# A chunked attention and two feed-forward layers: blocks cut by batch, additions on another engine, copies later

## The chip, the cores and the metric

The kernel runs on one core of a Trainium2 chip. Its engines are TensorE (PE; PEld is its weight load), VectorE (DVE), ScalarE (ACT), GpSimd (POOL) and SyncE (SP), which here only issues transfers. The metric is the device time of one execution in microseconds (us).

## The reference

For 8 batches, 8 heads, 576 tokens and 64 numbers a head, attention is computed within chunks of 64 tokens. Its output x, 4608 tokens by 512, goes through two feed-forward layers of width 2048. All is float32.

```python
scores = scale * np.matmul(q_c, k_c.transpose(0, 1, 2, 4, 3))
...
attn = attn / (np.sum(attn, axis=-1, keepdims=True) + 1e-09)
out = np.matmul(attn, v_c)
...
r = np.maximum(h, 0.0)
g = s * (r * r) + b
return (g @ w_out).astype(np.float32)
...
g = h * (1.0 / (1.0 + np.exp(-1.702 * h)))
return (g @ w_out).astype(np.float32)
```

## The kernel before

Every float32 operand is split into a high and a low part, and a product is three matmuls (high by high, high by low, low by high). `split` makes the parts: ScalarE copies the high one (L102), VectorE subtracts it (L103).

The 4608 tokens are cut into 9 blocks of 512. As a batch has 576 tokens, most blocks cross from one batch into the next, and `runs` gives the pieces. A block goes through attention in four pairs of heads (class `Pair`): loads of q and k (L294) and v (L304) on SP's queue, one for each run, transposes on VectorE (L311 for q and k, L320 for p), matmuls, and the softmax (mx L359, p L360 and L364, sm L366 to L368, p L369). L339 stores x of a block that comes later in a pair of blocks.

Blocks 0 to 6 then go singly through the first layer: `gemm_in` (matmuls L554; ScalarE's L566 takes h from PSUM, L567 squares it, L102 and L103 split it into gh and gl) and `gemm_out` (L629). One block goes singly through the second layer (L569 to L572 in place of L566 and L567). All others are computed in pairs of blocks by the class `Halves`, a scheme that needs 7 products in place of 8, in which some weight operands are sums of quarters of the weights. These sums lie in DRAM in `wi_sums` and `wo_sums`, together with copies of three quarters (`copies`, L263).

The second layer's weights come in 64 bits a number and are decoded by `decode_second`: integer operations on ScalarE, VectorE (L127, L130) and GpSimd (L128), a store to DRAM on GpSimd's queue (L203), then `add_quarters` (L221 to L224, four additions of 128x256), a split (ScalarE L209, VectorE L211) and stores on SP (L213). `sums` does the same for the first layer's weights (L240, `add_quarters`, L247, L252, stores L254). Both write their sums to a staging buffer `wst`, of which there are three. `second_weights` loads the decoded weights back (wm, L228) and splits them into resident buffers (ScalarE L150, VectorE L151).

The order is made in two steps. `at(t, f)` puts a piece of work on a list with a time t; 32 units are one block's stage, and the pieces are traced in the order of t. A scheduler then orders each engine's instructions by its own estimate. `behind` makes an instruction wait for a marked one. Each engine runs its instructions strictly in its order. SP has eight transfers in flight at most, since its transfers take eight semaphores in turn.

Of the kernel before, what the change touches and what calls it, by code (L numbers as in the profile page):

```python
# [11 lines left out]
ALU = mybir.AluOpType  # L12
# [4 lines left out]
P = 128  # L17
CH = 64
# [7 lines left out]
LAG = 2  # L26
# [11 lines left out]

PLACE = {"M1": 0, "M2": 1, "M4": 2, "M5": 3, "M6": 4, "M7": 5, "M3": 6}
BANK = {"M1": "x", "M6": "x", "M7": "x", "M4": "x", "M5": "d", "M3": "d", "M2": "b"}  # L40
PAIRS = ((1, 1), (0, 7), (1, 3), (1, 5), (1, 7))
OUT_ORDER = ("M1", "M5", "M6", "M2", "M7", "M3", "M4")


# [1 line left out]
def chunk_attention_two_ffn(ctx, tc, q, k, v, w1_in, w1_out, s, b, w2_in, w2_out, out):  # L46
# [17 lines left out]
    NB_MAX = 512  # L64
    sizes = [512] * 9
    assert sum(sizes) == NT
    starts = [sum(sizes[:i]) for i in range(len(sizes))]
    NBLK = len(sizes)
    PAIRED = [j + c for f, j in PAIRS if f == 0 for c in range(2)]
    SINGLE = NBLK - len(PAIRED)  # L70

    const = ctx.enter_context(tc.tile_pool(name="const", bufs=1))
# [142 lines left out]
    def add_quarters(kind, s, tiles):  # L215

        one, two = tiles
        a11, a22 = one[:, 0, :], two[:, 1, :]
        a12, a21 = (one[:, 1, :], two[:, 0, :]) if kind == "wi" else (two[:, 0, :], one[:, 1, :])
        s1, s2, s3, s4 = (s[:, t, :] for t in range(4))  # L220
        nc.gpsimd.tensor_tensor(out=s1, in0=a21, in1=a22, op=ALU.add)  # L221
        nc.gpsimd.tensor_tensor(out=s3, in0=a11, in1=a21, op=ALU.subtract)
        nc.gpsimd.tensor_tensor(out=s2, in0=s1, in1=a11, op=ALU.subtract)
        nc.gpsimd.tensor_tensor(out=s4, in0=a12, in1=s2, op=ALU.subtract)  # L224

    def second_weights(kind, i):
        m = tmp("wm")
# [37 lines left out]

    def runs(j):

        c0, n = starts[j] // CH, sizes[j] // CH
        done = 0
        while done < n:  # L270
            bb, c = divmod(c0 + done, CPB)
            step = min(n - done, CPB - c)
            yield done, step, bb, c
            done += step

    heads = [slice(h * CH, (h + 1) * CH) for h in range(2)]

    class Pair:
# [160 lines left out]
    class Early:  # L439
# [4 lines left out]
            self.raw, self.v = {}, {}  # L444

        def load(self, to, src, i, h0, nh):
            t0 = starts[self.j] + i * P
            done = 0
            while done < P:
                bb, t = divmod(t0 + done, S)  # L450
                n = min(P - done, S - t)
                nc.sync.dma_start(
                    out=to[done:done + n, h0 * D:(h0 + nh) * D].rearrange("p (h d) -> p h d", d=D),
                    in_=src[bb, h0:h0 + nh, t:t + n, :].rearrange("h p d -> p h d"),
                )
                done += n

        def load_qk(self, h0, nh):
            for x, src in (("q", q), ("k", k)):
# [65 lines left out]
        steps_at(((o - 2, 3), (o + 1, 1), (o + 2, 4), (o + 8, 1), (o + 8.5, 1)), pr.steps)  # L525

    def plan_y(j):
        base = NS * (SINGLE + j - 1)
        n = sizes[j]
        st = {}  # L530

        def load(m):
            st[m] = tmp("yst")[:, 0:n]
            nc.sync.dma_start(out=st[m], in_=y_dram[j][:, m, :])

        def sp(m):
# [77 lines left out]
    def gemm_out(f, j, i, g):  # L614
        n = sizes[j]
        gh, gl = g
        hi, lo = W[f, "wo", i]
        na = KD if f == 0 else n // P
        if i == 0:
            for m in range(na):  # L620
                acc[m] = acc_ps.tile([P, n if f == 0 else DM], F32, tag=f"acc{m}", name=f"acc{m}")
        for m in range(na):
            sl = slice(m * P, (m + 1) * P)
            if f == 0:
                prods = ((lo[:, sl], gh), (hi[:, sl], gh), (hi[:, sl], gl))
            else:
                prods = ((gl[:, sl], hi), (gh[:, sl], hi), (gh[:, sl], lo))
            for a, (l_, r_) in enumerate(prods):
                nc.tensor.matmul(  # L629
                    out=acc[m], lhsT=l_, rhs=r_, start=i == 0 and a == 0, stop=i == KF - 1 and a == 2  # L630
                )
        if i == KF - 1:
            if f == 0 and j == 0:
                make_shift()
            for m in range(na):
                w = n if f == 0 else DM
                st = tmp("ost")[:, 0:w]
                add = shift[:, m:m + 1]
                if f == 0 and m % 2:
                    nc.vector.tensor_scalar(  # L640
                        out=st, in0=acc[m], scalar1=s_ap, scalar2=add, op0=ALU.mult, op1=ALU.add
                    )
                elif f == 0:
                    nc.scalar.activation(out=st, in_=acc[m], func=AF.Identity, scale=s_ap, bias=add)
                elif m % 2:
                    nc.vector.tensor_copy(out=st, in_=acc[m])
                else:
                    nc.scalar.copy(out=st, in_=acc[m])
                if f == 0:
                    nc.sync.dma_start(out=y_dram[j][:, m, :], in_=st)  # L650
                else:
                    t0 = starts[j] + m * P
                    nc.sync.dma_start(out=out[t0:t0 + P, :], in_=st)


    HF, HK = KF // 2, KD // 2
# [4 lines left out]
    class Halves:  # L661


        def __init__(self, f, j, base):
            self.f, self.j, self.base = f, j, base
            self.last = (f, j) == PAIRS[-1]
            self.x, self.w, self.g, self.op, self.ps, self.kept = {}, {}, {}, {}, {}, {}


        def load_x(self, k):  # L670
            self.raw = getattr(self, "raw", {})
            for (a, c) in ((0, 0), (0, 1), (1, 1), (1, 0)):
                t = tmp("xr")
                nc.gpsimd.dma_start(out=t, in_=(y_dram if self.f else x_dram)[self.j + c][:, k + a * HK, :])  # L674
                self.raw[k, a, c] = t

        def x_place(self, n):
# [47 lines left out]
        def first(self, i, m):  # L725
            key = i, BANK[m]
            start = key not in self.ps
            if start:
                self.bank(key, BANK[m], f"acc{i % KD}")
            w = self.wi[i][PLACE[m]]  # L730
            for k in range(HK):
                xh, xl = self.x[m, k]
                hi, lo = w[:, k, 0, :], w[:, k, 1, :]
                for a, (l_, r_) in enumerate(((lo, xh), (hi, xh), (hi, xl))):
                    nc.tensor.matmul(  # L735
                        out=self.ps[key], lhsT=l_, rhs=r_,
                        start=start and k == 0 and a == 0, stop=k == HK - 1 and a == 2,
                        skip_group_check=not start,
                    )
            if m == "M4" and i == HF - 1:  # L740
                marks["last first product", self.f, self.j] = latest(mybir.EngineType.PE)

        def keep(self, key, name):
            self.kept[key[0], name] = t = tmp("kept")
# [80 lines left out]
        def second(self, n, i, zs=(0, 1)):  # L825
# [14 lines left out]
                        skip_group_check=not start,  # L840
                    )
            if n == 0 and i == 3:
                behind(old, mybir.EngineType.PE, ("last first product", self.f, self.j))

        def keep_out(self, z, bank, name):
            self.kept[z, name] = t = tmp("kept")
# [2 lines left out]
        def result(self, name, z):  # L849
# [7 lines left out]
            if self.f == 0:  # L857
                m = (int(name[0]) - 1) * HK + z
                y = tmp("ost")
                nc.scalar.activation(out=y, in_=c, func=AF.Identity, scale=s_ap, bias=shift[:, m:m + 1])  # L860
                nc.sync.dma_start(out=y_dram[self.j + int(name[1]) - 1][:, m, :], in_=y)
                return
            o = tmp("ost").rearrange("p (u l) -> p u l", l=BK)
            nc.vector.transpose(out=o, in_=c.rearrange("p (u l) -> p u l", l=BK))
            t0 = starts[self.j + int(name[1]) - 1]
# [99 lines left out]
    plan_first_products()  # L965
    for j in range(2, NBLK):
        plan_attention(j)
    plan_y(0)
# [5 lines left out]
    for i in range(KF):  # L974
        for n, kind in enumerate(("wi", "wo")):
            t = NS * (SINGLE - 1) + 2 * i + 1 + 3 * n
            at(t, second_weights, kind, i)
            if i >= KF // 2:
                at(t + 3, copies, 1, kind, i - KF // 2)
    def first_product(*a):  # L980
        G[a] = gemm_in(*a)

    for z in range(2, SINGLE + 1):
        f, j = divmod(z, SINGLE)
# [3 lines left out]
    for n, (f, j) in enumerate(PAIRS):  # L988
        Halves(f, j, NS * (SINGLE + 1) + 2 * LAG + 56 * n).plan()
# [33 lines left out]
```

## Time and profile before

| what | value |
|---|---|
| median of three runs | 1634.05 us (1632.6 to 1637.57) |
| the profiled execution's own time | 1637.07 us |
| its span | 1635.3 us |
| mean granted clock of TensorE | 0.985 |
| VectorE busy | 1126.0 us, 69% |
| ScalarE busy | 823.1 us, 50% |
| GpSimd busy | 252.0 us, 15% |

The span is the time from the first to the last instruction of the profiled execution. Busy times are sums over instructions. The granted clock is 1 at TensorE's higher level and 0.5 at its lower one. The times in the rows further down count from the span's start.

### The profile page before, as it was taken

The numbers are of one execution on the slowest core, as the hardware profiler recorded it, in microseconds if no ns is written. First come the engines' busy times: TensorE is split into PE (matmuls) and PEld (weight loads), VectorE is DVE, ScalarE is ACT, GpSimd is POOL, SyncE is SP. The second block draws the span as 40 slices with busy tenths as digits, with TensorE's granted clock in tenths as the row PEclk, the third lists the DMA queues.
The fourth block names the chain that finished last, engine by engine and source line by source line (L and its number), as shares of the span: only waits on it lengthen the run. The fifth ranks groups of instructions, "written<-read, shape, count | busy, mean of one in ns | idle before, by whom it ended". The sixth has DMA issues, their size and how long they took to land.

```text
span 1635.3 us, 24857 instructions
## 1 busy us (share of the span) xinstructions
PE 1584.5 (97%) x8840; PEld 1296.5 (79%) x8840; DVE 1126.0 (69%) x1836; ACT 823.1 (50%) x1427; POOL 252.0 (15%) x286
## 2 busy tenths in 40 slices
PE   7889998999999999999999999999999999999998
PEld 5668886778888888787888888888888888888886
DVE  5667668768777776766754697359468946984685
ACT  3766424445444555555233564776346525653552
POOL 1344214234333333200100000010001000100000
PEclk7999999999999999999999999999999999999999
DMA  9757667666665566799615777687668686877764
GB/s 231 227 171 206 202 170 216 167 178 173 186 173 160 165 203 162 231 284 294 189 47 163 222 252 196 201 270 212 204 194 273 184 220 210 259 199 207 217 202 76
DMA packets 392395, 326.73 MB, mean 200 GB/s; under 512 B 256592, under 2 KB 330320, under 8 KB 392272
## 3 DMA queue, kind: packets, MB, share of 16 engines
q1 hardware_dynamic: 382096, 301.81, 65.5%
q0 software_dynamic: 5760, 18.88, 3.4%
q10 hardware_dynamic: 4416, 4.46, 0.8%
q8 instruction: 70, 1.15, 0.3%
q14 instruction: 53, 0.43, 0.1%
HBM read 232.78 MB, written 92.27 MB: 199 GB/s over the span
## 4 chain that ended last, share of the span: by engine, by line
PE 52%; DVE 4%; DMA 3%; issue 1%; ACT 1%; SPq 1%; POOL 1%; DVEq 0%; POOLq 0%; ACTq 0%
PE x L735 13%; PE x L837 13%; PE d L735 7%; PE d L837 7%; PE b L837 3%; PE b L735 3%; PE acc L629 3%; PE h L554 3%; DMA wm<-w_wi 1%; DVE pt L320 1%; DMA wm<-w_wo 1%; DVE wi L151 0%; DVE gl L103 0%; SPq L263 0%; PE xT L330 0%
## 5 line engine op out<-in xcount | busy, mean ns | idle before, releaser
L554 PE MATMUL h<-xh,wi 128*128 128x512 f32 x1024 | 326.1, 400 | 18.3 <-ACT r L585 8.6
L629 PE MATMUL acc<-gh,wo 128*128 128x512 f32 x896 | 278.7, 395 | 3.5 <-ACT gh L102 3.5
L554 PEld LDWEIGHTS h<-xh,wi 128*128 128x128 f32 x1024 | 193.1, 192 | 61.5 <-ACT r L585 9.4
L554 PE MATMUL h<-xl,wi 128*128 128x512 f32 x512 | 202.4, 396 | 0.0
L629 PEld LDWEIGHTS acc<-gh,wo 128*128 128x128 f32 x896 | 167.4, 189 | 39.5 <-ACT gh L102 4.0
L629 PE MATMUL acc<-gl,wo 128*128 128x512 f32 x448 | 173.4, 393 | 2.4 <-DVE gl L103 2.4
L813 ACT ACTIVATE op<-wo 128x512 fp32r<-128x512 f32 x160 | 100.0, 630 | 101.4 <-PE x L837 34.4
L837 PE MATMUL x<-op,wi 128*128 128x512 f32 x540 | 130.2, 389 | 0.0
L735 PE MATMUL x<-xh,wi 128*128 128x512 f32 x400 | 124.1, 391 | 3.1 <-DVE wo L756 3.1
L814 DVE TENSOR_TENSOR op<-wo,op 128x512 fp32r<-128x512 f32 x160 | 108.5, 685 | 19.7 <-ACT op L813 18.1
L837 PEld LDWEIGHTS x<-op,wi 128*128 128x128 f32 x540 | 101.4, 188 | 21.0
L554 PEld LDWEIGHTS h<-xl,wi 128*128 128x128 f32 x512 | 98.1, 192 | 21.4 <-DVE xl L103 0.3
L659 DVE TENSOR_TENSOR wo<-wo 128x512 f32<-128x512 f32 x160 | 107.9, 687 | 4.5 <-ACT wo L759 3.7
L763 DVE TENSOR_TENSOR wo<-wo,r 128x512 f32<-128x512 f32 x96 | 66.0, 691 | 65.0 <-ACT r L762 64.6
L128 POOL TENSOR_TENSOR wm<-wm,wc 128x512 int32<-128x512 int32 x52 | 73.1, 1408 | 211.2 <-DVE wm L127 95.5
L674 POOL DMA_DIRECT2D xr<-y x32 | 17.5, 548 | 561.5 <-DVE op L814 274.4
L629 PEld LDWEIGHTS acc<-gl,wo 128*128 128x128 f32 x448 | 84.3, 189 | 21.6 <-DVE gl L103 3.9
L813 ACT ACTIVATE gh<-wo 128x512 fp32r<-128x512 f32 x120 | 75.1, 630 | 52.2 <-PE x L837 18.9
L320 DVE STREAM_TRANSPOSE pt<-p 32x256 f32<-32x256 f32 x224 | 97.6, 436 | 3.9
L762 ACT ACTIVATE r<-wo 128x512 f32<-128x512 f32 x96 | 60.7, 632 | 75.9 <-DVE wo L756 75.1
L814 DVE TENSOR_TENSOR gl<-wo,gh 128x512 fp32r<-128x512 f32 x120 | 80.9, 688 | 19.0 <-ACT gh L813 13.4
L735 PEld LDWEIGHTS x<-xh,wi 128*128 128x128 f32 x400 | 74.7, 188 | 20.4 <-DVE wo L756 5.2
(162 smaller groups left out, 3030.1 us busy)
## 6 DMA issues: line engine op xcount, KB each, us to landing
wi<-wo_sums SPq DMA_DIRECT2D x140, 512.0 KB, 4.3
wi<-wi_sums SPq DMA_DIRECT2D x120, 512.0 KB, 3.8
wst<-in_moe_w_out SPq DMA_DIRECT2D x32, 512.0 KB, 4.1
wst<-in_moe_w_in SPq DMA_DIRECT2D x24, 512.0 KB, 4.4
wi_sums<-wi SPq DMA_DIRECT2D x48, 256.0 KB, 4.0
wo_sums<-wo SPq DMA_DIRECT2D x48, 256.0 KB, 3.9
wi<-wi_sums SPq DMA_DIRECT2D x40, 256.0 KB, 3.6
y<-ost SPq DMA_DIRECT2D x36, 256.0 KB, 3.6
```

Of the source, the lines that this page charges most:

```text
L128: nc.gpsimd.tensor_tensor(out=t, in0=t, in1=c.bitcast(I32), op=ALU.add)
L320: nc.vector.transpose(out=pt[r.start + ek * BK:r.start + (ek + 1) * BK, :, eq * BK:(eq + 1) * BK], in_=p[r.start + eq * BK:r.start + (eq + ...
L554: nc.tensor.matmul(out=ps, lhsT=w_[:, kk, :], rhs=x_, start=kk == 0 and a == 0, stop=kk == KD - 1 and a == 2,)
L629: nc.tensor.matmul(out=acc[m], lhsT=l_, rhs=r_, start=i == 0 and a == 0, stop=i == KF - 1 and a == 2)
L659: nc.vector.tensor_tensor(out=to, in0=one, in1=two, op=ALU.subtract)
L674: nc.gpsimd.dma_start(out=t, in_=(y_dram if self.f else x_dram)[self.j + c][:, k + a * HK, :])
L735: nc.tensor.matmul(out=self.ps[key], lhsT=l_, rhs=r_, start=start and k == 0 and a == 0, stop=k == HK - 1 and a == 2, skip_group_check=not ...
L762: nc.scalar.activation(out=r, in_=h, func=AF.Sigmoid, scale=1.702)
L763: nc.vector.tensor_tensor(out=g, in0=h, in1=r, op=ALU.mult)
L813: nc.scalar.activation(out=hi, in_=src, func=AF.Copy)
L814: nc.vector.tensor_tensor(out=lo, in0=src, in1=hi.bitcast(F32), op=ALU.subtract)
L837: nc.tensor.matmul(out=self.ps[key], lhsT=l_, rhs=r_, start=start and i == 0 and a == 0, stop=i == HF - 1 and a == 2, skip_group_check=not ...
```

## The change

The change has three parts.

1. Blocks are cut otherwise. Block 1 (`LEFT`) takes the last chunk of each batch, eight runs of one chunk; each other block is the first 512 tokens of one batch, one run. A pair of heads in blocks 2 to 7 is loaded with 10 transfers in place of 20, of the same bytes in all: 6 blocks by 4 pairs by 10 are 240 issues fewer on SP. Block 1, loaded at the program's start, takes 24 transfers of 64 rows in place of 15. Block 1, not block 0, goes singly through the second layer, and its result is stored in pieces of 64 rows.
2. The four additions of `add_quarters` run on VectorE, not on GpSimd. It is called 32 times.
3. The 48 copies of the second layer's weights (256 KB each) are no longer made as the weights come in, but in the stage after, in four groups of 12; each group waits on SP behind the store of block 8's x for one pair of heads.

A line n of the kernel before is line n + 1 or a little more after.

```diff
-PAIRS = ((1, 1), (0, 7), (1, 3), (1, 5), (1, 7))
+PAIRS = ((1, (0, 2)), (0, (7, 8)), (1, (3, 4)), (1, (5, 6)), (1, (7, 8)))
...
+    LEFT = 1
...
-        nc.gpsimd.tensor_tensor(out=s1, in0=a21, in1=a22, op=ALU.add)
-        nc.gpsimd.tensor_tensor(out=s3, in0=a11, in1=a21, op=ALU.subtract)
-        nc.gpsimd.tensor_tensor(out=s2, in0=s1, in1=a11, op=ALU.subtract)
-        nc.gpsimd.tensor_tensor(out=s4, in0=a12, in1=s2, op=ALU.subtract)
+        nc.vector.tensor_tensor(out=s1, in0=a21, in1=a22, op=ALU.add)
+        nc.vector.tensor_tensor(out=s3, in0=a11, in1=a21, op=ALU.subtract)
+        nc.vector.tensor_tensor(out=s2, in0=s1, in1=a11, op=ALU.subtract)
+        nc.vector.tensor_tensor(out=s4, in0=a12, in1=s2, op=ALU.subtract)
...
-        c0, n = starts[j] // CH, sizes[j] // CH
-        done = 0
-        while done < n:
-            bb, c = divmod(c0 + done, CPB)
-            step = min(n - done, CPB - c)
-            yield done, step, bb, c
-            done += step
+        if j == LEFT:
+            for bb in range(B):
+                yield bb, 1, bb, CPB - 1
+        else:
+            yield 0, NB_MAX // CH, first_batch(j), 0
+
+    def first_batch(j):
+        return j - (j > LEFT)
...
+                marks["stored", self.j, self.hp] = latest(mybir.EngineType.SP)
...
-                    t0 = starts[j] + m * P
-                    nc.sync.dma_start(out=out[t0:t0 + P, :], in_=st)
+                    for r, bb in zip(heads, (2 * m, 2 * m + 1)):
+                        t0 = bb * S + NB_MAX
+                        nc.sync.dma_start(out=out[t0:t0 + CH, :], in_=st[r])
...
-            if i >= KF // 2:
-                at(t + 3, copies, 1, kind, i - KF // 2)
+    for n, (kind, i) in enumerate((kind, i) for kind in ("wi", "wo") for i in range(KF // 2)):
+
+        def later(kind=kind, i=i, p=n // HP):
+            old = len(nc.cur_bb.bb.instructions)
+            copies(1, kind, i)
+            behind(old, mybir.EngineType.SP, ("stored", NBLK - 1, p))
+        at(NS * SINGLE + 7 * (n // HP) + 5.6 + 0.1 * (n % HP), later)
```

The order on VectorE, at the ninth of the 16 decodes (kind wi), where L211 splits the sums of the second layer and the sums of the first layer follow; gl, xl, mx and p belong to the blocks' work. Before:

```order
L103 TENSOR_TENSOR gl<-r,gh 128x512 [waits PE_49,Activation_49]
L211 TENSOR_TENSOR wst<-wst 128x1024 [waits Activation_49]
L103 TENSOR_TENSOR gl<-r,gh 128x512 [waits PE_49,Activation_49]
L103 TENSOR_TENSOR xl<-xT,xh 128x512 [waits Activation_49]
L359 TENSOR_REDUCE mx<-sc 128x8 [waits PE_49]
L360 TENSOR_TENSOR p<-sc,mx 128x512 [waits DMAHW6_49,DVE_49]
L366 TENSOR_REDUCE sm<-p 128x8 [waits Activation_49]
L252 TENSOR_TENSOR wst<-wst,vs 128x512 [waits DMAHW1_49,Activation_49,Pool_49]
```

And now:

```order
L225 TENSOR_TENSOR wst<-wm,wst 128x256 [waits DVE_49]
L212 TENSOR_TENSOR wst<-wst 128x1024 [waits Activation_49]
L104 TENSOR_TENSOR gl<-r,gh 128x512 [waits PE_49,Activation_49]
L222 TENSOR_TENSOR wst<-vs 128x256 [waits DMAHW4_49,DVE_49]
L223 TENSOR_TENSOR wst<-vs 128x256
L224 TENSOR_TENSOR wst<-wst,vs 128x256 [waits DVE_49]
L104 TENSOR_TENSOR xl<-xT,xh 128x512 [waits Activation_49]
L362 TENSOR_REDUCE mx<-sc 128x8 [waits PE_49]
L225 TENSOR_TENSOR wst<-vs,wst 128x256 [waits DVE_49]
L253 TENSOR_TENSOR wst<-wst,vs 128x512 [waits DVE_49,Activation_49]
```

The additions L222 to L225 now stand in this queue; the first of them waits for a transfer (DMAHW4), the store of the staging buffer that L212 wrote two rows ahead, and xl, mx and all behind stand after it.

The order on SP where the second weights are loaded, from the last store of the last sums on; w_wo_117 is the second of the output weights' tiles. Before:

```order
L254 DMA wo_sums_148<-wst 128x2x256
L294 DMA ks<-in_k 32x14x32
L339 DMA x_150<-xo 128x512
L294 DMA ks<-in_k 32x14x32 x2
L294 DMA qs<-in_q 32x2x32 x4
L294 DMA ks<-in_k 32x2x32 x4
L304 DMA vs<-in_v 64x7x64 x2
L304 DMA vs<-in_v 64x64
L228 DMA wm<-w_wo_117 128x512
L228 DMA wm<-w_wi_103 128x512
```

And now:

```order
L255 DMA wo_sums_148<-wst 128x2x256
L341 DMA x_150<-xo 128x512
L296 DMA ks<-in_k 32x16x32
L306 DMA vs<-in_v 64x8x64 x6
L229 DMA wm<-w_wo_117 128x512
L229 DMA wm<-w_wi_103 128x512
```

The loads of the second run of each block are gone from ahead of the weights' loads, and the weights stand nearer to the stores.

## Rows read from the trace of the kernel before

**Rows 1.** The page's part on engines: busy us (share of the span) xinstructions.

```profile
PE 1584.5 (97%) x8840; PEld 1296.5 (79%) x8840; DVE 1126.0 (69%) x1836; ACT 823.1 (50%) x1427; POOL 252.0 (15%) x286
```

**Rows 2.** PE's waits in 255 to 400 us: us in total, times, longest.

```profile
PE h L554 <- ACT r L566: 7.1, 3, 4.4
PE acc L629 <- DVE gl L103: 2.4, 2, 1.4
```

**Rows 3.** PE's waits in 661 to 775 us.

```profile
PE acc L629 <- ACT gh L102: 3.5, 1, 3.5
PE h L554 <- DVE r L570: 1.5, 1, 1.5
PE xT L330 <- DVE pt L320: 0.9, 1, 0.9
```

**Rows 4.** Windows: length, busy us of PE, PEld, DVE, ACT, POOL, clock, DMA share, GB/s.

```profile
275.00:300.00 25.00, 20.62 (x133) 15.88 (x133) 24.54 (x30) 10.55 (x18) 12.50 (x15) 0.86 0.75 198
287.20:294.10 6.90, 4.92 (x12) 3.86 (x13) 6.62 (x15) 3.67 (x7) 0.00 (x0) 0.51 0.87 246
686.60:693.40 6.80, 6.10 (x24) 4.36 (x26) 6.64 (x10) 4.07 (x8) 2.66 (x4) 0.50 0.93 267
693.40:768.50 75.10, 73.14 (x482) 59.61 (x478) 46.99 (x85) 38.81 (x67) 2.30 (x2) 1.00 1.03 298
768.50:775.30 6.80, 6.02 (x24) 4.40 (x25) 5.77 (x10) 4.12 (x8) 0.00 (x0) 0.50 0.77 207
775.00:850.00 75.00, 75.00 (x512) 61.90 (x509) 47.67 (x86) 23.50 (x41) 4.40 (x8) 1.00 0.44 136
```

**Rows 5.** Timeline of VectorE, 276 to 288 us: start, length, instruction.

```profile
276.76 4.23 DVE L103 TENSOR_TENSOR gl<-r,gh 128x512 fp32r<-128x512 f32 x1
...
287.29 0.69 DVE L360 TENSOR_TENSOR p<-sc,mx 128x512 f32<-128x512 f32 x1
```

**Rows 6.** Timeline of ScalarE at 285 us, idle time before in brackets.

```profile
285.54 1.06 ACT L209 ACTIVATE wst<-wst 128x1024 fp32r<-128x1024 f32 x1 [3.95 <-POOL wst L224]
```

**Rows 7.** VectorE's instructions grouped by form: count, busy us, mean ns.

```profile
L814 DVE TENSOR_TENSOR gl<-wo,gh 128x512 fp32r<-128x512 f32 x120 | 80.9, 688 | 19.0 <-ACT gh L813 13.4 <-PE x L837 3.7 <-PE b L837 0.7
L103 DVE TENSOR_TENSOR gl<-r,gh 128x512 fp32r<-128x512 f32 x80 | 70.9, 890 | 9.7 <-ACT gh L102 9.6
...
L103 DVE TENSOR_TENSOR xl<-xT,xh 128x256 fp32r<-128x256 f32 x16 | 6.3, 417 | 4.2 <-ACT xh L102 4.2
```

**Rows 8.** Timeline of ScalarE at 686 us.

```profile
686.10 0.63 ACT L150 ACTIVATE wo<-wm 128x512 fp32r<-128x512 f32 x1 [4.75 <-DMA wm<-w_wo]
```

**Rows 9.** Timeline of SP, 674 to 683 us: issues.

```profile
674.58 0.51 SPq L294 DMA_DIRECT2D ks<-in_k  x1
...
682.90 0.53 SPq L228 DMA_DIRECT2D wm<-w_wo  x1
```

**Rows 10.** The copies' line L263 in 650 to 775 us.

```profile
L263 SPq DMA_DIRECT2D wi_sums<-wi x24: 359/514/1172, 685.0 to 770.1; - x24
L263 SPq DMA_DIRECT2D wo_sums<-wo x22: 360/468/1290, 700.7 to 773.3; - x22
```

**Rows 11.** Windows, the loads of block 1 at the start.

```profile
24.40:43.60 19.20, 16.00 (x186) 12.25 (x183) 13.61 (x29) 8.41 (x19) 2.97 (x2) 0.73 1.10 240
```

**Rows 12.** GpSimd's integer additions, grouped by form.

```profile
L128 POOL TENSOR_TENSOR wm<-wm,wc 128x512 int32<-128x512 int32 x52 | 73.1, 1408 | 211.2 <-DVE wm L127 95.5 <-ACT r L567 28.2 <-ACT wc L125 20.0
```

**Rows 13.** GpSimd's waits in 230 to 700 us.

```profile
POOL wst L221 <- DMA wi_sums<-wst: 53.3, 7, 9.6
POOL wst L221 <- DMA wo_sums<-wst: 52.9, 7, 9.5
```

**Rows 14.** Transfers by kind: count, KB each, median us from issue to landing.

```profile
wi_sums<-wst SPq DMA_DIRECT2D x16, 512.0 KB, 3.2
wo_sums<-wst SPq DMA_DIRECT2D x16, 512.0 KB, 3.5
```

**Rows 15.** Timeline of PE at 282 us.

```profile
282.40 0.39 PE L629 MATMUL acc<-gl,wo 128*128 128x512 f32 x1
```

More of the change, by code (lines that the diff above doesn't have):

```diff
@@ L66, in chunk_attention_two_ffn @@
     assert sum(sizes) == NT
-    starts = [sum(sizes[:i]) for i in range(len(sizes))]
     NBLK = len(sizes)
-    PAIRED = [j + c for f, j in PAIRS if f == 0 for c in range(2)]
+    assert B * CH == NB_MAX and S == NB_MAX + CH and NBLK == B + 1
+    LEFT = 1
+    PAIRED = [j for f, blocks in PAIRS if f == 0 for j in blocks]
     SINGLE = NBLK - len(PAIRED)
@@ L446, in load @@
         def load(self, to, src, i, h0, nh):
[L447 to L451, printed above, removed]
+            for off, m, bb, c in runs(self.j):
+                lo, hi = max(off * CH, i * P), min((off + m) * CH, (i + 1) * P)
+                if lo >= hi:
+                    continue
+                t = c * CH + lo - off * CH
                 nc.sync.dma_start(
-                    out=to[done:done + n, h0 * D:(h0 + nh) * D].rearrange("p (h d) -> p h d", d=D),
-                    in_=src[bb, h0:h0 + nh, t:t + n, :].rearrange("h p d -> p h d"),
+                    out=to[lo - i * P:hi - i * P, h0 * D:(h0 + nh) * D].rearrange("p (h d) -> p h d", d=D),
+                    in_=src[bb, h0:h0 + nh, t:t + hi - lo, :].rearrange("h p d -> p h d"),
                 )
-                done += n
         def load_qk(self, h0, nh):
@@ L527, in plan_y @@
     def plan_y(j):
-        base = NS * (SINGLE + j - 1)
+        base = NS * (SINGLE - 1)
         n = sizes[j]
@@ L661, in chunk_attention_two_ffn, with __init__ @@
     class Halves:
-        def __init__(self, f, j, base):
-            self.f, self.j, self.base = f, j, base
-            self.last = (f, j) == PAIRS[-1]
+        def __init__(self, f, blocks, base):
+            self.f, self.blocks, self.base = f, blocks, base
+            self.last = (f, blocks) == PAIRS[-1]
             self.x, self.w, self.g, self.op, self.ps, self.kept = {}, {}, {}, {}, {}, {}
@@ L673, in load_x @@
                 t = tmp("xr")
-                nc.gpsimd.dma_start(out=t, in_=(y_dram if self.f else x_dram)[self.j + c][:, k + a * HK, :])
+                nc.gpsimd.dma_start(out=t, in_=(y_dram if self.f else x_dram)[self.blocks[c]][:, k + a * HK, :])
                 self.raw[k, a, c] = t
@@ L740, in first @@
             if m == "M4" and i == HF - 1:
-                marks["last first product", self.f, self.j] = latest(mybir.EngineType.PE)
+                marks["last first product", self.f, self.blocks] = latest(mybir.EngineType.PE)
         def keep(self, key, name):
@@ L842, in second @@
             if n == 0 and i == 3:
-                behind(old, mybir.EngineType.PE, ("last first product", self.f, self.j))
+                behind(old, mybir.EngineType.PE, ("last first product", self.f, self.blocks))
         def keep_out(self, z, bank, name):
@@ L860, in result @@
                 nc.scalar.activation(out=y, in_=c, func=AF.Identity, scale=s_ap, bias=shift[:, m:m + 1])
-                nc.sync.dma_start(out=y_dram[self.j + int(name[1]) - 1][:, m, :], in_=y)
+                nc.sync.dma_start(out=y_dram[self.blocks[int(name[1]) - 1]][:, m, :], in_=y)
                 return
@@ L864, in result @@
             nc.vector.transpose(out=o, in_=c.rearrange("p (u l) -> p u l", l=BK))
-            t0 = starts[self.j + int(name[1]) - 1]
+            t0 = first_batch(self.blocks[int(name[1]) - 1]) * S
             f0 = ((int(name[0]) - 1) * HK + z) * P
@@ L967, in chunk_attention_two_ffn @@
         plan_attention(j)
-    plan_y(0)
+    plan_y(LEFT)
     for n, (i, kind) in enumerate((i, kind) for i in range(KF // 2) for kind in ("wi", "wo")):
@@ L983, in chunk_attention_two_ffn @@
     for z in range(2, SINGLE + 1):
-        f, j = divmod(z, SINGLE)
+        f, j = (0, z) if z < SINGLE else (1, LEFT)
         for i in range(KF):
@@ L987, in chunk_attention_two_ffn @@
             at(NS * z + 2 * (i + LAG) + 1.6, lambda *a: gemm_out(*a, G.pop(a)), f, j, i)
-    for n, (f, j) in enumerate(PAIRS):
-        Halves(f, j, NS * (SINGLE + 1) + 2 * LAG + 56 * n).plan()
+    for n, (f, blocks) in enumerate(PAIRS):
+        Halves(f, blocks, NS * (SINGLE + 1) + 2 * LAG + 56 * n).plan()
     traced, last = nc.cur_bb.bb.instructions, None
```

## The prediction

> **What bounds the kernel now.** The first view is the page's table of engines: TensorE (PE) works 1584.5 of 1635.3 us [rows 1]. So all that a change of order and of queues can give is its idle time, 1635.3 − 1584.5 = 51 us, and the time that PE runs at the lower of its two clock levels. The next view is therefore the list of what PE waited for, stage by stage.
>
> Two stages carry it. In 255 to 400 us, where the second weights are decoded and the sums made beside the blocks' attention, PE waits 7.1 us for ScalarE's L566, 4.4 of them at one place, and 2.4 us for VectorE's L103 [rows 2]. In 661 to 775 us, where the second weights are loaded into SBUF, it waits 3.5 us for ScalarE's L102, and 1.5 and 0.9 us for VectorE (L570, L320) [rows 3]. The windows add a cost of a second kind: in 287.2–294.1, 686.6–693.4 and 768.5–775.3, each just behind such an idle stretch, the granted clock is 0.50 to 0.51, the 1.2 GHz level, and not 1.00 [rows 4]. PE's busy time there is 4.92, 6.10 and 6.02 us, of which half would be saved at 2.4 GHz: 2.5, 3.05 and 3.0 us.
>
> So the losses are: first stage 7.1 + 2.4 + 2.5 = 12.0 us; second stage 3.5 + 1.5 + 0.9 + 3.05 + 3.0 = 12.0 us. Together 24 us, 1.5% of the kernel, is the most that the change can give in the middle of the program; what is left of the 51 us lies before 255 us and after 775 us.
>
> What ends those waits? First stage: at 276.76 VectorE's L103, a subtraction of 128x512 with two operands, took 4.23 us, and all behind it in its queue came later, up to p at 287.29 [rows 5]. ScalarE stood 3.95 us at L209 for the addition L224 on GpSimd (POOL), until 285.54 [rows 6], and then for that late p; L566 stands behind both in its queue, and PE behind L566. That GpSimd is what makes VectorE slow is read from the groups by form: L103 gl takes 890 ns on average beside POOL's work, and the same subtraction, L814 gl, 688 ns in the pairs, where POOL computes nothing [rows 7]. Second stage: ScalarE stood 4.75 us for the second weight wm<-w_wo, until 686.10 [rows 8]; its load was issued at 682.90, and the run of SP issues ahead of it starts at 674.58 [rows 9]. Of the issues in 650–775 us, 46 are copies L263 [rows 10], and DMA is busy at 1.03 in 693.4–768.5 [rows 4].
>
> **The change, part by part.**
>
> *One run per load, copies held.* In order's listing of SP, 15 issues stand between the sums' last store L254 and the load w_wo_117 before, 8 after. They took 682.90 − 674.58 = 8.32 us for 15 [rows 9], 0.555 us each; seven fewer bring the load 3.9 us forward, which is more than the 3.5 us that PE waited [rows 3]. The half-clock stretch behind it goes as well: 3.5 + 3.05. For the places at 767–775 us: 46 copies of 0.262 MB, 12.1 MB, leave the stage. In 693.4–768.5 the DMA engines moved 298 GB/s × 75.1 us = 22.4 MB at a share of 1.03 [rows 4]; without most of the copies the share falls to about a half, so I count the 1.5 + 0.9 + 3.0 as gone too, less 1 us for what is left of them. Part A: −11 us (bounds 0, if the waits only move, and −12.0).
>
> The copies return in 775–850, where the share is 0.44 at 136 GB/s [rows 4]. 12.6 MB more in 75 us is 168 GB/s, 304 in all, and by the same ratio a share of 0.98. There is room, but no more than that. Each group of 12 copies waits on SP behind a store of block 8's x, and the first pair's weight loads stand behind the groups. 12 × 0.555 = 6.7 us is the most a load comes later per group; those loads fill a ring of buffers that PE reaches only after this stage. I take 0 (bounds 0 and one such delay with its half clock, 6.7 + 3 = +9.7).
>
> At the start, 15 loads of block 1 become 24 of the same bytes. Nine more issues are 9 × 0.555 = 5 us if issuing were the limit; but DMA is busy at 1.10 in 24.4–43.6 [rows 11], so the bytes are. I take 0 (bounds −2, for pieces that can be used sooner, and +5).
>
> The 240 issues that SP saves and the other order of blocks cost PE nothing: it gets the same matmuls. The eight out stores of 64 rows instead of four of 128 lie beside the pairs' work.
>
> *Additions on VectorE.* There are 128 of them, each 128x256. VectorE has run none; its nearest row, a subtraction of 128x256, takes 417 ns [rows 7]. So 128 × 0.417 = 53 us come onto VectorE. It gets back between nothing and 80 × (890 − 688) = 16 us on gl [rows 7], since POOL keeps its integer additions L128, 52 × 1408 ns = 73 us in all [rows 12]. A net 37 to 53 us over the 450 us from 250 to 700 is 8 to 12% of VectorE's time. It has that, except where it is full already (24.54 of 25 in 275–300 [rows 4]), and there the 4.23 us instruction fills it. As throughput the price is 0, hidden beside PE's matmuls; if the cover were gone, all 37 to 53 us would be PE's.
>
> What the rows show of contention is the 202 ns per gl. The Trainium skill ("SBUF — State Buffer", section "SBUF: two separate sides") states that VectorE and GpSimd share a port pair as an exclusive lock, which a VectorE instruction with two SBUF inputs takes against a GpSimd one that reads SBUF. By it the moved additions, having two SBUF inputs, would themselves be held by each L128 that runs beside them: at most 52 × 1.408 = 73 us more on VectorE, which would make it full in stretches; by the rows' mean of 202 ns it is not. No row here shows a 128x256 addition of VectorE beside L128.
>
> The gain: at 289 us p comes earlier by most of the 3.5 us (4.23 − 0.69) and L209 no longer waits for POOL, so PE's 4.4 us and the half clock behind it, 2.5, go: −6.9 us. The other 2.7 us for L566 and the 2.4 for L103 [rows 2] I leave as they are.
>
> The cost: a new wait. The sums' additions write a staging buffer that the decode's store has just been reading. Before, POOL stood for that store's landing, 7 + 7 times, 53.3 + 52.9 us [rows 13]. After, VectorE stands, with gl, mx, p and pt behind it. How long? POOL's mean, 106.2/14 = 7.6 us, is a bound from above, since it had little else to do; from below, such a store of 512 KB lands 3.2 or 3.5 us after its issue (median) [rows 14], less what VectorE does meanwhile. In order's listing of VectorE, 7 places have only one to three instructions of 0.7 us between the store's source and the addition, 2 are half covered, 6 are covered by transposes. So VectorE stands between 3.2 − 3 × 0.7 = 1.1 and 7.6 − 0.7 = 6.9 us at 7 to 9 places; nearer to the stores' own row I take 2.7, some 19 us at the 7. Does this reach PE? At 276.76 a delay of 3.5 us in L103 did not stop it at once: gl ended at 280.99 and PE's first use of it is at 282.40 [rows 15]. So I take one place of nine to hit in full, 2.7 + 3.0 (a half-clock stretch [rows 4]) = +5.7. Part B: −6.9 + 5.7 = −1.2 (bounds −12.0 with no hit and all waits gone, and nine hits, 51 − 6.9 = +44).
>
> **Sum.** −11 − 1.2 = −12.2 us. The profiled execution took 1637.07 us for a span of 1635.3, and lies 3.0 above the median of 1634.05, so it would become 1624.9; against the median the forecast is 1622. The own range of this case is 1614 to 1629.
>
> **The rivals.**
>
> *Full gain.* No place of the nine reaches PE, and the waits for L103 go as well: −24 us, 1610. For it: PE's slack of 1.4 us behind the slow gl [rows 15]. Against it: VectorE is fuller and has a new wait.
>
> *No change.* The loads L228 come no earlier, because they wait for free buffers, or the copies make the first pair late by what they gave: A = 0, B = −1.2, so 1633. For it: a share of 0.98 in 775–850 leaves no room. Against it: 3.9 us of issues are gone from the place that cost 3.5 + 3.05.
>
> *Slower.* VectorE's standing for stores reaches PE at 5.7 us a place. The other terms are −11 − 6.9 = −17.9, so from the fourth place on the change loses; at five it is 5 × 5.7 − 17.9 = +10.6, 1645. For it: 7 tight places, and PE's gaps of 2.4 us for gl already [rows 2]. Against it: that slack again [rows 15], and that 3.5 us on VectorE cost nothing at once there. The Trainium skill ("Perfetto Trace Analysis", section "Optimizing Scalar/DVE Operations") speaks for this side: where VectorE is saturated, it has work moved off it, to GpSimd too. The trace has VectorE saturated in one stretch of 25 us, and by that stretch's cause it is GpSimd's company that fills it.
>
> **Chances.** Forecast 0.55, full gain 0.13, no change 0.18, slower 0.14. What the measurement can tell from no change is 0.3%, 4.9 us. Faster by more: 0.55 + 0.13 + a share of "no change" that ends below 1629, 0.72; same 0.15; slower 0.13. The range of 8 in 10 takes in full gain and no change and leaves the slower end out: 1608 to 1638.
>
> **What would show it.** PE's waits in 661–775 all under 1 us, and no clock of 0.5 there; the issue of w_wo_117 some 4 us sooner against its consumer; DMA share near 0.5 in 693–768 and near 1 in 775–850; gl near 0.7–0.75 us; additions of 0.35–0.42 us on VectorE; VectorE idle before L222 on "DMA wi_sums<-wst" some 19 us in all. Wrong would make it: PE gaps of 2 us and more for gl or p behind those waits at four or more places, with half-clock stretches; or a wait at the first pair for wi<-wi_sums.

## The result, and the profile after

The changed kernel takes 1617.87 us (median of four runs, 1617.15 to 1619.40), the kernel before on the same chip 1635.54: a ratio of 0.9891, 95% interval 0.9878 to 0.9904, so 17.7 us less. 1622 was forecast, with a range of 1608 to 1638. The profiled execution has a span of 1616.7 us, 18.6 less than before.

The page's table of engines answers to [rows 1]:

```profile
PE 1576.2 (97%) x8840; PEld 1293.6 (80%) x8840; DVE 1153.2 (71%) x1964; ACT 826.0 (51%) x1427; POOL 153.4 (9%) x158
```

VectorE has 27 us more work, GpSimd 99 us less. PE's waits in 255 to 400 us, the first stage:

```profile
PE h L556 <- ACT r L568: 1.3, 1, 1.3
PE acc L631 <- DVE gl L104: 1.2, 1, 1.2
```

9.5 us of [rows 2] have become 2.5. In 661 to 775 us, the second stage, the list of PE's waits is empty; all of [rows 3] is gone. The windows (length, busy us of PE, PEld, DVE, ACT, POOL, clock, DMA share, GB/s):

```profile
275.00:300.00 25.00, 23.67 (x158) 18.58 (x155) 21.85 (x43) 12.66 (x23) 0.00 (x0) 1.00 0.85 240
650.00:693.00 43.00, 43.00 (x300) 35.64 (x299) 33.31 (x59) 24.58 (x43) 4.08 (x4) 1.00 0.86 234
693.40:768.50 75.10, 75.09 (x490) 61.31 (x489) 56.02 (x105) 39.17 (x67) 2.20 (x4) 1.00 0.63 177
775.00:850.00 75.00, 75.00 (x465) 61.73 (x464) 43.59 (x76) 25.10 (x44) 2.18 (x4) 1.00 0.67 218
```

PE works without a pause and at the upper clock level from 650 to 850 us. DMA in 693.4–768.5 fell from 1.03 [rows 4] to 0.63, and rose in 775–850 from 0.44 to 0.67 only: the held copies run from 757 to 830 us, 12 of the 48 ahead of 768 us, since the whole stage comes earlier. To see how much each stage gave I compared the times at which the two kernels start the same number of matmuls. At the 1600th (246 us) the changed kernel is 0.5 us ahead (this lead swings by 1 us within ten matmuls), at the 2400th (376 us) 11.2, at the 4400th (683 us) 7.0, at the 5200th (816 us) 19.4, and 19.3 at the last matmul. So the first stage gives some 10.7 us, the stretch behind it takes 4.2 back, and the second stage gives 12.4. VectorE by form:

```profile
L817 DVE TENSOR_TENSOR gl<-wo,gh 128x512 fp32r<-128x512 f32 x120 | 80.8, 686 | 19.0 <-ACT gh L816 13.4 <-PE x L840 3.7 <-PE b L840 0.7
...
L104 DVE TENSOR_TENSOR gl<-r,gh 128x512 fp32r<-128x512 f32 x80 | 59.5, 745 | 11.2 <-ACT gh L103 11.1
...
L225 DVE TENSOR_TENSOR wst<-vs,wst 128x256 f32<-128x256 f32 x16 | 6.7, 421 | 0.3
...
L222 DVE TENSOR_TENSOR wst<-wm 128x256 f32<-128x256 f32 x16 | 6.7, 417 | 0.3
```

gl fell from 890 [rows 7] to 745 ns, an addition takes 0.42 us. VectorE's waits for the decodes' stores, which were GpSimd's [rows 13]:

```profile
DVE wst L222 <- DMA wi_sums<-wst: 10.2, 4, 4.7
DVE wst L222 <- DMA wo_sums<-wst: 10.1, 5, 3.0
```

That is 20.3 us at 9 places, where some 19 us at 7 to 9 were forecast.

### The profile page after: what moved, and what is told of

Same layout as the page of the kernel before. It is cut to its first block, busy times and chain, and to the rows that moved or that the text cites. A ratio compares the mean times of both kernels' runs of the same rounds, so it can differ in the third digit from the quotient of the medians.

```text
span 1616.7 us, 24597 instructions
## 1 busy us (share of the span) xinstructions
PE 1576.2 (97%) x8840; PEld 1293.6 (80%) x8840; DVE 1153.2 (71%) x1964; ACT 826.0 (51%) x1427; POOL 153.4 (9%) x158
## 3 DMA queue, kind: packets, MB, share of 16 engines
q8 instruction: 70, 1.15, 0.3%
## 4 chain that ended last, share of the span: by engine, by line
PE 86%; DVE 5%; DMA 3%; SPq 2%; ACT 2%; issue 2%; POOL 0%; DVEq 0%; POOLq 0%; ACTq 0%
PE acc L631 18%; PE h L556 17%; PE x L738 14%; PE x L840 13%; PE d L738 7%; PE d L840 7%; PE b L840 3%; PE b L738 3%; SPq L455 2%; PE sc L354 2%; PE xT L332 2%; DVE pt L322 1%; DMA wo_sums<-wst 1%; DVE wm L131 1%; DMA wi_sums<-vs 1%
## 5 line engine op out<-in xcount | busy, mean ns | idle before, releaser
L556 PE MATMUL h<-xh,wi 128*128 128x512 f32 x1024 | 322.8, 397 | 10.1 <-ACT r L587 7.7
L129 POOL TENSOR_TENSOR wm<-wm,wc 128x512 int32<-128x512 int32 x52 | 74.6, 1438 | 447.8 <-DVE wm L128 197.8
L738 PEld LDWEIGHTS x<-xh,wi 128*128 128x128 f32 x400 | 74.7, 188 | 20.3 <-DVE wo L759 5.2
L840 PE MATMUL x<-gh,wi 128*128 128x512 f32 x280 | 80.5, 389 | 0.0
```

What stands on the lines that cost most here:

```text
L129: nc.gpsimd.tensor_tensor(out=t, in0=t, in1=c.bitcast(I32), op=ALU.add)
L556: nc.tensor.matmul(out=ps, lhsT=w_[:, kk, :], rhs=x_, start=kk == 0 and a == 0, stop=kk == KD - 1 and a == 2,)
L738: nc.tensor.matmul(out=self.ps[key], lhsT=l_, rhs=r_, start=start and k == 0 and a == 0, stop=k == HK - 1 and a == 2, skip_group_check=not ...
L840: nc.tensor.matmul(out=self.ps[key], lhsT=l_, rhs=r_, start=start and i == 0 and a == 0, stop=i == HF - 1 and a == 2, skip_group_check=not ...
```

## Experiments

Each was timed in five rounds beside the kernel before; ratios are to that kernel, with 95% intervals. Four ran on one chip at a time. A part that is done or undone also gives the scheduler other work to order, so each order differs in more than the part named.

**The additions alone.** Only this in the kernel before:

```diff
-        nc.gpsimd.tensor_tensor(out=s1, in0=a21, in1=a22, op=ALU.add)
+        nc.vector.tensor_tensor(out=s1, in0=a21, in1=a22, op=ALU.add)
...
```

> The kernel before with the additions on VectorE alone. Theory (each part pays in its own stage): the first stage's 7.0 us, that the changed kernel is ahead by at 680 us, come from the additions, so 1635.5 - 7 = 1628.5 us, and PE's waits of 3.5, 0.9 and 1.5 us in the second stage stay, with both half-clock stretches. Rival (the first stage gains because SP issues fewer loads): no gain, 1633 to 1638, and a PE wait of 4 us or so near 289 us stays.

Measured: 1638.24 against 1638.03 us, ratio 1.0003 (0.9992 to 1.0014). The theory fails on the time. PE's waits in 255 to 400 us:

```profile
PE h L554 <- ACT r L566: 6.0, 2, 3.0
PE acc L629 <- DVE gl L103: 3.0, 2, 2.7
PE xT L330 <- DMA vs<-in_v: 1.2, 3, 0.5
```

10.2 us, no fewer than before. The wait for L566 near 289 us fell from 4.4 to 3.0, but the one at 268 us is 3.0 us now where it was 2.0, and gl at 343 us costs 2.7 where it cost 1.4. ScalarE's rows just before the one at 268 us, first in the kernel before, then now:

```profile
260.95 0.63 ACT L364 ACTIVATE p<-p 128x512 f32<-128x512 f32 x1 [8.68 <-DVE p L360]
261.48 1.04 ACT L209 ACTIVATE wst<-wst 128x1024 fp32r<-128x1024 f32 x1
```

```profile
261.48 1.06 ACT L209 ACTIVATE wst<-wst 128x1024 fp32r<-128x1024 f32 x1 [6.49 <-DVE wst L224]
265.16 0.63 ACT L364 ACTIVATE p<-p 128x512 f32<-128x512 f32 x1 [2.62 <-DVE p L360]
```

Before, p stood ahead of L209 here. Now L209 stands first and waits for VectorE's addition, and p behind it: what stood in GpSimd's queue stands in VectorE's. Later, waits of 1.5 us for pt (425 us) and 1.0 for gl (596) come on top. In the second stage:

```profile
PE acc L629 <- DVE gl L103: 2.3, 2, 1.6
PE h L554 <- DVE r L570: 1.5, 1, 1.5
PE h L554 <- ACT r L566: 1.0, 1, 1.0
```

The 3.5 us wait for ScalarE is gone, and so are both half-clock stretches: at the 4400th matmul this kernel is 8.1 us behind (2.7 of them already at the 1600th, ahead of the first stage), at the 5200th 1.6. What is lost comes back in the second stage, which neither side expected: the weight load for which ScalarE let PE wait 3.5 us before lands at 689.8 us, 3.8 later than before, and PE comes 8.1 later.

**The cut alone.** The changed kernel with additions on GpSimd and copies early:

```diff
-        nc.vector.tensor_tensor(out=s1, in0=a21, in1=a22, op=ALU.add)
+        nc.gpsimd.tensor_tensor(out=s1, in0=a21, in1=a22, op=ALU.add)
...
+            if i >= KF // 2:
+                at(t + 3, copies, 1, kind, i - KF // 2)
```

> The blocks cut by batch alone; additions on GpSimd, copies early. Theory: the load w_wo_117 comes 3.9 us sooner, so PE's 3.5 us wait at 687 us and its half clock go, the place at 768 us stays: -6.5 us, 1629. Rival (either SP part alone frees the second stage): -12.4, 1623. Rival (the first stage gains from fewer loads): a further -7 in 255 to 400 us, 1616 to 1622.

Measured: 1624.65 us, ratio 0.9924 (0.9908 to 0.9940), the largest part of the gain. PE's waits in the first stage, then in the second:

```profile
PE h L556 <- ACT r L568: 4.6, 1, 4.6
PE acc L631 <- DVE gl L104: 0.4, 1, 0.4
```

```profile
PE h L556 <- DVE r L572: 1.5, 1, 1.5
PE h L556 <- ACT r L568: 0.9, 1, 0.9
```

The large wait near 289 us is as it was (4.6 us), but 2.7 us for L566 and 2.0 of the 2.4 for gl have gone. At the 4400th matmul this kernel is 5.3 us ahead, so the rival (the first stage gains from fewer loads) holds, though with 5.3 us and not 7, and not at 289 us. In the second stage the place at 687 us is gone, and at 758 us 1.5 us are left without a half-clock stretch; 8.4 us are gained there. VectorE's rows show the way in the first stage. Before:

```profile
247.47 0.69 DVE L103 TENSOR_TENSOR xl<-xT,xh 128x512 fp32r<-128x512 f32 x1 [5.91 <-ACT xh L102]
...
248.68 0.71 DVE L311 STREAM_TRANSPOSE qt<-qs 128x512 f32<-128x512 f32 x1
...
259.50 0.69 DVE L359 TENSOR_REDUCE mx<-sc 128x8 f32<-128x512 f32 x1 [2.65 <-PE sc L351]
```

With the cut:

```profile
243.03 0.71 DVE L313 STREAM_TRANSPOSE qt<-qs 128x512 f32<-128x512 f32 x1
...
255.41 0.69 DVE L362 TENSOR_REDUCE mx<-sc 128x8 f32<-128x512 f32 x1 [3.78 <-PE sc L354]
```

q's transpose no longer stands behind xl, which waits 5.91 us for ScalarE. It starts 5.6 us earlier, and mx finds its scores 4.1 us earlier; so p, and ScalarE's L566 behind it, are no longer late at 264 us.

**The copies held, alone.**

```diff
-            if i >= KF // 2:
-                at(t + 3, copies, 1, kind, i - KF // 2)
+    for n, (kind, i) in enumerate((kind, i) for kind in ("wi", "wo") for i in range(KF // 2)):
...
+            behind(old, mybir.EngineType.SP, ("stored", NBLK - 1, p))
```

> The copies held, alone; blocks and additions as before. Theory: the place at 767 to 775 us loses its 2.4 us of waits and 3.0 us of half clock, the one at 687 us stays since its load is queued behind q, k and v loads: -5.4 us, 1630. Rival (either SP part alone frees the second stage): -12.4, 1623. Rival (the copies only move the crowding to the next stage): no gain, 1635, with PE waiting near 850 us.

Measured: 1629.97 us, ratio 0.9952 (0.9939 to 0.9966), −7.9 us by the ratio. PE's waits in 640 to 775 us:

```profile
PE acc L630 <- ACT gh L102: 3.0, 1, 3.0
```

The place at 767 us is gone as the theory has it, and the one at 687 stays. That it gave 2.5 us more than 5.4 fits the clock: the wait is 3.0 us, not 3.5, and no half-clock stretch stands behind it. The first stage has no gain: 0.2 us ahead at 683 us.

**Cut and copies, additions on GpSimd.** The changed kernel with the four lines of `add_quarters` back on GpSimd.

> The changed kernel with its additions back on GpSimd. Theory: only the second stage's gain, -12.4 us, 1623, and PE's wait of about 4 us near 289 us is back, with its half clock. Rival (fewer SP issues are what the first stage gains by): 1616 to 1619, like the changed kernel.

Measured: 1620.04 us, ratio 0.9894 (0.9879 to 0.9909), 0.0003 from the changed kernel's: the rival. In the first stage:

```profile
PE h L556 <- ACT r L568: 4.6, 1, 4.6
PE acc L631 <- DVE gl L104: 0.8, 1, 0.8
```

The wait of 4.6 us is back as the theory expected, and the clock behind it:

```profile
285.00:288.40 3.40, 3.40 (x10) 2.61 (x9) 3.21 (x9) 1.85 (x4) 0.00 (x0) 0.50 0.94 270
```

PE ran 3.4 us at half clock, 1.7 us lost. So at their own place the additions do what was forecast, some 5 us, and yet the whole is worth 1: at the 4400th matmul this kernel is 5.8 us ahead, the changed one 7.0.

**Cut and additions, copies early.**

```diff
+            if i >= KF // 2:
+                at(t + 3, copies, 1, kind, i - KF // 2)
```

> The changed kernel with its copies early again (blocks cut, additions on VectorE). Theory now (the cut is the main part, it frees both stages; the additions give 1 us, and the held copies clear what is left in the second stage): 13.4 + 1 = 14 us under the kernel before, a place near 758 us with a PE wait of 1.5 us and perhaps a half clock stays. Rival (with the additions on VectorE the second stage is clear without holding the copies, since in the run of the additions alone it gained 6.4 us): 18 us under, as the changed kernel.

Measured: 1622.55 us, ratio 0.9923 (0.9910 to 0.9936), 12.6 us. The theory holds: waits of 0.6 us for pt and 1.6 for r near 757 us, and 3.4 us of half clock.

**Additions and copies held, blocks as before.**

> Additions on VectorE and copies held, blocks cut as before. Theory (the additions lose some 5 us in the first stage while SP still issues two loads per run, since VectorE then stands for late loads and stores; the second stage is clear): 8 us under the kernel before, PE waits of 2 to 3 us near 268, 293 and 343 us. Rival (the additions pay by themselves, and only the crowded second stage hid it): 14 us under or more.

Measured: 1629.94 us, ratio 0.9967 (0.9956 to 0.9979), 5.4 us, less than the copies alone, though their intervals overlap. The theory's side: PE waits 3.0 us at 266 and 3.2 at 291. The 2.7 us at 343 did not come.

**Each load in two halves.** The changed kernel, same bytes, 240 issues more:

```diff
+        elif LEFT < j < NBLK - 1:
+            for c in (0, 4):
+                yield c, 4, first_batch(j), c
```

> The changed kernel with each load of blocks 2 to 7 issued in two halves: the same bytes and the same blocks, 240 issues more on SP. Theory (the cut pays through the number of issues, each some 0.5 us on SP): it falls back to what additions and held copies give without the cut, 1630 us, with PE waits of about 3 us near 268 and 290 us. Rival (the cut pays by its other order of blocks): 1617 to 1620, like the changed kernel.

Measured: 1629.46 us, ratio 0.9964 (0.9951 to 0.9976), within 0.5 us of the last kernel, which has the old blocks. So the cut pays by the number of issues, with what order the scheduler makes of it, and not by its order of blocks. PE's waits in 255 to 400 us:

```profile
PE h L559 <- ACT r L571: 6.5, 2, 3.5
PE acc L634 <- DVE gl L104: 2.3, 2, 1.3
```

They are at 266, 290, 340 and 395 us, places much like those before.

**Sums in other buffers.** The changed kernel, `sums` writing to two buffers of the pool `tmp`:

```diff
-        s = staged().rearrange("p f z -> p (f z)").bitcast(F32).rearrange("p (t c) -> p t c", c=2 * P)
-        add_quarters(kind, s, q)
+        part2 = [tmp("sum").rearrange("p (t c) -> p t c", c=2 * P) for _ in range(2)]
+        add_quarters(kind, [part2[t // 2][:, t % 2, :] for t in range(4)], q)
```

> The changed kernel with the first layer's sums written to two buffers of the pool tmp, not to the staging buffer that the decode's store still reads; the work is the same. Theory (VectorE's 20 us of standing for stores cost PE only part of its four waits of 5.0 us in all): VectorE's waits for wi_sums and wo_sums under 8 us, PE's four waits shrink by 1 to 4 us, 1614 to 1617. Rival (those PE waits come from the rows of p and pt that stand behind sums work in VectorE's queue, not from the store): 1617 to 1619, same PE waits. Rival (the pool tmp runs short): slower than 1620.

Measured: 1620.93 us, ratio 0.9913 (0.9901 to 0.9925): some 3 us over the changed kernel by the ratios, at the edge of what they can tell, and not the theory's gain. VectorE's 20 us of waits for stores are gone, and the waits at 384, 410 and 527 us with them: at the 4400th matmul this kernel is 8.2 us ahead, 1.2 more than the changed one. But the wait near 283 us grew to 3.3 us, with 3.4 us of half clock behind it, and the second stage has a new one:

```profile
PE acc L631 <- DVE gl L104: 2.8, 2, 2.3
```

So taking the store waits away gave PE little, and in this manner costs more elsewhere.

**More work on GpSimd.** The changed kernel with 128 additions that nobody waits for:

```diff
+        for n in range(8):
+            m = ms[n % 2]
+            nc.gpsimd.tensor_tensor(out=wo_total[:, :2 * P], in0=m[:, 0, :], in1=m[:, 1, :], op=ALU.add)
```

> The changed kernel with 128 further additions of 128x256 on GpSimd that nobody waits for (8 behind each decode, read from the decoded tiles, written to a spent tile). Theory (what hurt was GpSimd's running beside VectorE, an engine effect): gl goes back from 752 to 850 ns or more in 250 to 700 us and PE's waits in 255 to 400 us grow by 3 us or more, with a half-clock stretch: 1621 to 1626. Rival (what hurt was that ScalarE and VectorE waited for additions that stood in GpSimd's queue): gl slows too, but the time stays within 1.5 us of the changed kernel's.

Measured: 1648.84 us, ratio 1.0090 (1.0075 to 1.0105), 31 us over the changed kernel by the medians. The theory, and more than it expected. VectorE's additions by form, one group that runs beside the extra ones and one that does not:

```profile
L227 DVE TENSOR_TENSOR wst<-wst,wm 128x256 f32<-128x256 f32 x16 | 13.5, 843 | 0.2
...
L228 DVE TENSOR_TENSOR wst<-vs,wst 128x256 f32<-128x256 f32 x16 | 6.7, 421 | 0.3
```

An addition of the same size takes 843 ns in company and 421 without; gl takes 841 ns in 250 to 700 us, and VectorE's busy time is 1196.3 us, 43 more than in the changed kernel. No instruction in the trace waits for the extra additions themselves. PE's waits:

```profile
PE h L559 <- ACT r L571: 7.8, 1, 7.8
PE acc L634 <- DVE ost L645: 2.6, 1, 2.6
```

Between 280 and 550 us the clock is at its lower level in four stretches of 3.4 to 10.2 us. One thing is mixed in: the extra additions stand ahead of L129 in GpSimd's queue. VectorE's waits for L129 are 15.3 us against 13.2, so that is the smaller part.

**The additions divided.** Of the changed kernel, with `add_quarters` given an engine:

```diff
-        add_quarters(kind, s, q)
+        add_quarters(nc.gpsimd, kind, s, q)
```

> The changed kernel with the additions of decode_second on VectorE and those of sums, which wait for the store, on GpSimd. Theory (both costs count, so take the cheap half of each): VectorE no longer stands 20 us for stores, ScalarE's L210 doesn't wait for GpSimd; PE's waits near 282, 384, 410 and 527 us shrink, 1 to 3 us under the changed kernel. Rival (GpSimd's company costs more than the standing): 1 to 5 us over it.

Measured: 1619.57 us, ratio 0.9900 (0.9887 to 0.9914); the changed kernel, run again on this chip, took 1618.30. There is no gain, so the theory fails; the 1.3 us by which it is slower lie within the intervals. VectorE doesn't stand for stores, but gl is slower (810 ns in 250 to 700 us, 752 in the changed kernel), and ScalarE's L568 lets PE wait at 286 us:

```profile
L104 DVE TENSOR_TENSOR gl<-r,gh 128x512 fp32r<-128x512 f32 x71 | 57.3, 810 | 14.6 <-ACT gh L103 14.1 <-PE acc L631 0.5
```

```profile
PE h L556 <- ACT r L568: 3.8, 1, 3.8
```

The other way round:

```diff
-        add_quarters(kind, s, ms)
+        add_quarters(nc.gpsimd, kind, s, ms)
```

> The changed kernel with the additions of decode_second on GpSimd and those of sums on VectorE. Theory: both costs are kept, GpSimd's company at 270 to 285 us with the PE wait of 4.5 us, and VectorE's standing: 1 to 4 us over the changed kernel. Rival: the same time within 1 us, since neither cost reaches PE often.

Measured: 1624.39 us, ratio 0.9933 (0.9920 to 0.9947), 6.1 us over the changed kernel, beyond what the theory expected; PE's wait near 283 us is 2.9 us, and waits of 0.9 to 1.5 us stand at five places more.

**The changed kernel again.**

> The changed kernel once more, on the chip of the three others, to compare them with it: 17 to 19 us under the kernel before.

Measured: 1618.30 us, ratio 0.9896 (0.9881 to 0.9911). No kernel tried was faster.

The parts side by side, in us by the ratio on 1635.5 us, each with an interval of some ±2 us:

| parts | change |
|---|---|
| additions | +0.5 |
| cut | −12.4 |
| copies held | −7.9 |
| cut, additions | −12.6 |
| additions, copies | −5.4 |
| cut, copies | −17.3 |
| all three | −17.8 |

## Why the prediction was right, and where not

**Second stage, −11 forecast, −12.4 measured.** Right in size, and both places and both half-clock stretches went. The way to it was in part another. The issues ahead of the load w_wo_117 are seven fewer, but they take 5.8 us in place of 8.3, 2.5 less and not 3.9:

```profile
665.52 0.82 SPq L341 DMA_DIRECT2D x<-xo  x1
...
671.36 0.49 SPq L229 DMA_DIRECT2D wm<-w_wo  x1
```

ScalarE still stands 3.3 us for this load. But the gh that PE needs next stands ahead of it in ScalarE's queue, where before it stood behind L150 [rows 8]. Before, then the changed kernel, then the cut alone:

```profile
686.64 0.61 ACT L102 ACTIVATE gh<-r 128x512 fp32r<-128x512 f32 x1
```

```profile
671.66 0.63 ACT L103 ACTIVATE gh<-r 128x512 fp32r<-128x512 f32 x1
675.56 0.63 ACT L151 ACTIVATE wo<-wm 128x512 fp32r<-128x512 f32 x1 [3.27 <-DMA wm<-w_wo]
```

```profile
678.97 0.63 ACT L103 ACTIVATE gh<-r 128x512 fp32r<-128x512 f32 x1
682.63 0.63 ACT L151 ACTIVATE wo<-wm 128x512 fp32r<-128x512 f32 x1 [3.03 <-DMA wm<-w_wo]
```

In the cut alone it can't be the load's time: early copies stand among the issues, which take 10.1 us, and the load lands 5.4 us behind the 4400th matmul, where it landed 3.5 behind before; there the order is what is left. In the changed kernel the load lands with that matmul, so either may have done it, and which is not shown. Nor do the parts divide as in the working: the cut alone gave 8.4 us in this stage (6.55 forecast), the copies alone 9.1 (5.4), together more than the 12.4, since each of them took both half-clock stretches. The 1 us kept for what would be left was not needed.

**First stage, −1.2 forecast, −6.5 measured (10.7 less 4.2).** This is the term that was mis-sized, and the cause was wrong in one half. "The other 2.7 us for L566 and the 2.4 for L103 [rows 2] I leave as they are" failed: the cut took 2.7 of the one and 2.0 of the other. "The 240 issues that SP saves … cost PE nothing" was true as a cost, but they were given no gain outside the second stage, and that is where they had one. Two halves per load bring the waits back. So the total came out within the range, but 5.3 us of it (the cut alone, at the 4400th matmul) come from a place where the working had nothing, which is luck and not foresight.

**The wait at 289 us, −6.9 forecast.** Right in direction. In the changed kernel it is 1.3 us without a half-clock stretch, in the one with additions on GpSimd 4.6 and 1.7 us of clock: 5.0 us. What is left of it shows how:

```profile
276.62 1.06 ACT L210 ACTIVATE wst<-wst 128x1024 fp32r<-128x1024 f32 x1 [1.15 <-issue]
280.76 0.63 ACT L367 ACTIVATE p<-p 128x512 f32<-128x512 f32 x1 [3.08 <-DVE p L363]
```

L210 stood 1.15 us, not 3.95 [rows 6], but p still came late, since VectorE now does eight additions in that stretch.

**VectorE's waits for stores, +5.7 forecast.** Their length, 20.3 us, was right. Their price was too high: no place of nine cost 2.7 + 3.0. PE waited 1.2 us for gl at 384 us, 1.5 for pt at 410 and 1.0 for gl at 527, without a half-clock stretch in this execution, 3.6 us in all. The kernel with other buffers has none of these three waits, but another order too, so that the stores alone make them is likely and not shown.

**The net of the additions.** Forecast: −1.2. With the cut and the copies it is −0.5 by the ratios, with the cut −0.2, alone +0.5, with the copies +2.5; none of these can be told from 0, nor their sign. What the traces show is one place: with the old blocks the wait near 266 us is 2.0 us without the moved additions and 3.0 with them, with the new blocks it is gone in either case.

**No price as throughput.** Held: VectorE is at 21.85 us of 25 in 275–300 us, from 24.54. That L103's slowness came from GpSimd's company is shown, and not only argued, when the gl are taken one by one from the timelines of the two engines. In the kernel before, the 51 beside which GpSimd computed nothing took 682 ns on average and 695 at most, the other 29 took 1255; in the changed kernel 64 took 682 and 16 took 994. The one of 4.23 us [rows 5] lies beside four instructions of GpSimd, one right behind the other, and ends 0.56 us after the last of them.

The Trainium skill ("SBUF — State Buffer", section "SBUF: two separate sides") has VectorE and GpSimd share a port pair as an exclusive lock. By it the moved additions, with two inputs in SBUF, would be held by GpSimd's integer additions. The changed kernel hardly tests this: its groups of additions average 416 to 421 ns, but only one of the 128 ran beside an L129, for 0.11 us. In the run of the additions alone one began 0.1 us behind an L128 and took 1.48 us in place of 0.42, as the rule has it:

```profile
279.71 1.30 POOL L128 TENSOR_TENSOR wm<-wm,wc 128x512 int32<-128x512 int32 x1 [0.37 <-issue]
```

```profile
279.81 1.48 DVE L223 TENSOR_TENSOR wst<-wst,vs 128x256 f32<-128x256 f32 x1
```

**The rivals.** −17.7 lies about midway between full gain (−24, chance 0.13) and the forecast's −12.2. "No change" and "slower" did not come; the DMA share in 775–850 was 0.67, not 0.98, so the copies had room.

What stays open: whether the 240 issues act by their time on SP or by the order that the scheduler makes of the program without them. Near 245 us VectorE's queue has q's transpose ahead of xl in all eight kernels with one load per pair and tensor part, and behind it in all five with two. At this place it is the order: before, q and k had landed by 239.7 us, 9 us ahead of their transpose, and in the changed kernel by 230.6, 12 us ahead, so that in neither a load held it. For the other places it is not known, since no run has the fewer issues without the other order.

## What to carry to other kernels

Fewer issues on a queue can pay in a stage where no wait names a transfer, since a scheduler orders the other engines' work anew without them. At two places followed here (264 us, and 687 us in the cut alone) it was not a load that came sooner, but another instruction that stood ahead in VectorE's or ScalarE's queue. So read at each late instruction what stands in front of it in its own queue. A wait for a slow engine's result does not go away by moving the work to a faster one; it moves into that engine's queue, and pays only if the queue has room at that place. Price a new stand-still of an engine by what its consumers had in hand: here 20 us of it cost PE 3.6 us at most, in the execution that was profiled.

## What was not expected of the hardware

128 additions of GpSimd that nobody waits for, 116 us of its time, cost 31 us of the whole: VectorE's instructions beside them took up to twice their time by their groups' means (421 to 843 ns), and PE's longer waits brought half-clock stretches with them. A single subtraction on VectorE took 4.23 us in place of 0.68 beside four GpSimd instructions in a row. And a half-clock stretch after a PE wait is not sure: a wait of 3.0 us at 687 us had none behind it, one of 4.6 had 3.4 us, one of 3.5 had 6.8, and one of 1.5 us at 408 us was followed by 3.4 us in one execution of the changed kernel and by none in another.
